# Start addresses and slot places of the MLP operands in an attention-then-two-MLPs kernel

## The chip, the core and the metric

One core of one Trainium2 chip runs the whole program. The metric is the device time of one execution in microseconds (us), as the median of several runs. Smaller is better.

## What is computed

The inputs are q, k and v of shape (4, 8, 576, 64) and four weight matrices. An attention with a feature map comes first, then two MLPs over 2,304 rows of 512 columns:

```python
def phi(x):
    proj = einsum('bhsd,df->bhsf', x, w_phi)
    proj = proj - max(abs(proj), axis=-1)
    return concatenate([exp(proj), exp(-proj)])
kv = einsum('bhsf,bhsd->bhfd', phi(k), v);  z = sum(phi(k), axis=2)
x = einsum('bhsf,bhfd->bhsd', phi(q), kv) / (phi(q) . z + 1e-06)     # (2304, 512)
h = x @ w1_in;  x = where(h > 0, h, exp(min(h, 0)) - 1) @ w1_out       # 512 -> 2048 -> 512
h = x @ w2_in;  out = (h * clip(h + 3, 0, 6) / 6) @ w2_out             # 512 -> 2048 -> 512
```

The MLP weights arrive as 64-bit floats and are turned into 32-bit floats on the chip. Every MLP product is made of three matmuls of the fp32r type on a high and a low part of each operand: high x high, low x high, high x low.

## The kernel before

**Order of work.** Nothing runs in the order of the source. Every piece of work is a `Step` with an engine, a duration that the program assumes, its predecessors, a rank, and tokens of rings (buffers). `in_order` plays them through and emits the instructions of each engine in the order that comes out. The engines then run their own queues in that order, and wait for each other by semaphores.

**Attention.** Eight units (`unit(u)`), each for two heads and two batches. A unit projects k and q in runs of eight tiles (`projs`, L312), subtracts the row maximum on DVE (L322, L336), exponentiates on ACT (L345, L408), sums keys times values on PE (L370), transposes q on PE (L395), multiplies (L429) and divides, with the quotient written into `x32` by POOL (`scale`, L476). All these matmuls are plain fp32. Each of L312, L370 and L429 stands in the trace as two matmul records per call.

**MLPs.** The 2,304 rows are cut into blocks: b = 0 to 3 have 512 rows, b = 4 has 256. The 16 slices f of 128 hidden columns are taken in groups of four (`M1_GROUPS`, `M2_GROUPS`): for each group all five blocks, for each block the four slices. One item is `hid` (L732, 12 matmuls into `ps_p`), then `act1`, `gate`, `gate_hi`, `gate_lo` on ACT and DVE (tiles `e`, `g`, `gh`, `gl`), then `outp` (L794, 12 matmuls, 6 in the second MLP for b = 4). On PE the `outp` of an item stands behind the `hid` of the next one. In `hid` the weights are the stationary operand and x the moving one. In `outp` of the first MLP the weights are stationary and `gh`, `gl` move; in the second MLP `gh`, `gl` are stationary and the weights move.

**Weights.** Slice w (0 to 31 over both MLPs) lives in slot j = w % 6, as `w_h` and `w_l` of 2 x 512 columns. `fetch` loads half a slice, DVE turns it into 32-bit parts in eight steps (`to_f32`, L661 to L673), POOL adds the last part (L678) into one of four `w_b` buffers, and `w_hi` (L700) and `w_lo` (L706) on POOL write the slot and free the buffer.

**Memory.** Tiles lie behind each other in the order in which pools are opened. Slots 0 and 1 are in `wra`, which is open from the start. Slots 2 and 3 are in `mlp_a`, which takes the place of `att_a` once its last user is done (`open_a`); slots 4 and 5 are in `mlp_b`, which takes the place of `att_b` (`open_b`).

```python
SLOT = ["wra", "wra", "a", "a", "b", "b"]
```

`xh` and `xl` of blocks 1 to 4 are tiles of KD x n columns (`new_x`), those of block 0 lie in the buffers of raw q and k (`first_x`). In the built program the starts, in bytes of a partition, are these (all starts of one row agree modulo 128):

| tiles | start modulo 128 |
|---|---|
| `w_h`, `w_l` of slots 0, 1, 4, 5; x of blocks 2, 3, 4 | 32 |
| `w_h`, `w_l` of slots 2, 3; x of blocks 0, 1; `gh`, `gl` | 96 |
| `e` and `st` of the attention (operands of L429) | 64 |
| `kp` of the attention (stationary operand of L370) | 96 |

Of the kernel before, what the change touches and what calls it, by code (L numbers as in the profile page):

```python
# [7 lines left out]

F32 = mybir.dt.float32
F32R = mybir.dt.float32r  # L10
I32 = mybir.dt.int32
I64 = mybir.dt.int64
AF = mybir.ActivationFunctionType
ALU = mybir.AluOpType
AX = mybir.AxisListType
# [122 lines left out]
def attention_then_two_mlps(  # L138
# [28 lines left out]
    B, S, D = 4, 576, 64  # L167
    NF = w_phi.shape[1] // 2
    NT, DM = out.shape
    DFF = w1_out.shape[0]  # L170
    R = S // 64
    KD = DM // 128
    FT = DFF // 128
# [32 lines left out]
    ov = x32.rearrange("p (t n) -> p t n", n=DM)  # L206
    half_c = const.tile([128, 1], F32, name="half_c")
    nc.gpsimd.memset(half_c, 0.5)


    sb = ExitStack()
# [383 lines left out]
    def open_a():  # L595
        sa.close()
        pools["a"] = ctx.enter_context(tc.tile_pool(name="mlp_a", bufs=1, side="right"))
        new_x("a", 1)

    def open_b():  # L600
        sb.close()
        pools["b"] = ctx.enter_context(tc.tile_pool(name="mlp_b", bufs=1))
        for b in range(2, NB):
            new_x("b", b)

    X = {}

    def new_x(pool_, b):
        t = [
            pools[pool_].tile([128, KD, blocks[b][1]], F32R, name=f"x{part}{b}") for part in "hl"  # L610
        ]
        X[b] = tuple([t_[:, kk] for kk in range(KD)] for t_ in t)

    def first_x():

        t = [
            [rawp.tile([128, 2, 512], F32R, tag=s_, name=f"x{part}0{i}") for i in range(2)]
            for part, s_ in (("h", "k"), ("l", "q"))
        ]
        X[0] = tuple([t_[kk // 2][:, kk % 2] for kk in range(KD)] for t_ in t)  # L620

    def y_open():
        pass
# [8 lines left out]
    }  # L632

    W, F = {}, {}
    SLOT = ["wra", "wra", "a", "a", "b", "b"]
    pools["wra"] = wra
    for j in range(len(SLOT)):
        rings[f"w{j}"] = 1
    rings.update({"s": 2, "ca": 1, "cb": WB, "el_e": 2, "el_r": 1, "el_g": 2, "el_gh": GB, "el_gl": GB,
                  "y0": 1, "y1": 1, "y2": 1, "y3": 1})  # L640

    def fetch(w, i):
        m, f = divmod(w, FT)
        w_in, w_out = ((w1_in, w1_out), (w2_in, w2_out))[m]
        s = stg.tile([128, 512], I64, tag="s", name="w64", bufs=2)
        if i == 0:
            nc.sync.dma_start(out=s, in_=w_in[f])
        else:
            nc.sync.dma_start(out=s, in_=w_out[f * 128:(f + 1) * 128, :])
        F[w, i] = s  # L650

    def to_f32(w, i):
# [86 lines left out]
    def act1(m, b, f):  # L739
        n = blocks[b][1]  # L740
        el = pools["a"]
        ps = H[m, b, f]
        e = el.tile([128, 512], F32, tag="e", name="e", bufs=2)
        if m == 0:
            r_ = el.tile([128, 512], F32, tag="r", name="r")
            nc.scalar.activation(out=r_[:, :n], in_=ps[:, :n], func=AF.Relu, scale=-1.0)  # L746
            nc.scalar.activation(out=e[:, :n], in_=r_[:, :n], func=AF.Exp, scale=-1.0)
        else:
            nc.scalar.activation(  # L749
                out=e[:, :n], in_=ps[:, :n], func=AF.Relu, scale=1.0 / 6.0, bias=half_c  # L750
            )
        G[m, b, f] = e
# [80 lines left out]
    for w in range(2 * FT):  # L833
        j = w % len(SLOT)
        WT[w] = Token(f"w{j}")
        for i in range(2):
# [1 line left out]
            ts_, ta, tb = Token("s"), Token("ca"), Token("cb")  # L838
            x = step("SP", 1.4, bind_(fetch, w, i), takes=[ts_], rank=lead - 5, behind=[chain] if chain else [])
            chain = x  # L840
            cost = [0.6, 0.33, 0.33, 0.33, 0.6, 0.6, 0.6, 0.31]
            fns = to_f32(w, i)
            for n_, (us, fn) in enumerate(zip(cost, fns)):
                x = step(
# [73 lines left out]
    for it in seq:  # L918
        m, begins, ends, fi, fn, b, f = it
        n = blocks[b][1]  # L920
        tp, te, tr, tg, th, tl = (Token(x) for x in ("p", "el_e", "el_r", "el_g", "el_gh", "el_gl"))
        gtok[m, b, f] = (th, tl)
        ready = xr[b] if m == 0 else [nexts[b, kk] for kk in range(KD)]
        s = step("PE", 12 * pe1(n), bind_(hid, m, b, f), after=[WL[m * FT + f, 0], *ready], rank=clock, takes=[tp],
                 uses=[WT[m * FT + f]])
        s.behind += [x for x in hids.get("last", [])]
        hids["last"] = [s]
        hids.setdefault((m, b), []).append(s)
        clock += 12 * pe1(n)
        when = clock  # L930
        s = step("ACT", act(n) * (1 + (m == 0)), bind_(act1, m, b, f), after=[s, OPEN["a"]], rank=when, uses=[tp],
                 takes=[te, tr] if m == 0 else [te])
        if m == 0:
            tr.users.append(s)
        s = step("DVE", dve(n), bind_(gate, m, b, f), after=[s], rank=when, uses=[te, tp], takes=[tg])
        s = step("ACT", act(n), bind_(gate_hi, m, b, f), after=[s], rank=when, takes=[th], uses=[tg])
        gl_of[m, b, f] = step("DVE", dve(n), bind_(gate_lo, m, b, f), after=[s], rank=when, takes=[tl], uses=[tg],
                              port=True)
        if prev is not None:
            put_outp(*prev, clock)  # L940
            clock += 12 * pe1(blocks[prev[5]][1])
        prev = it
# [16 lines left out]
def _laid_out(name, a):  # L959
# [7 lines left out]
    elif name == "w_phi":  # L967
        a = np.block([[a, np.zeros_like(a)], [np.zeros_like(a), a]])
    elif name.endswith("w_in"):
        a = a.reshape(4, 128, 16, 128).transpose(2, 1, 0, 3).reshape(16, 128, 512)  # L970
    return np.ascontiguousarray(a)


# [21 lines left out]
```

## Time and profile before

| | |
|---|---|
| median of 3 runs | 1015.91 us (1015.71 to 1016.2) |
| the profiled execution | 1015.86 us |
| its span | 1014.0 us |
| granted TensorE clock over the span | 0.998 |
| PE busy | 994.8 us |
| DVE / ACT / POOL busy | 728.0 / 422.2 / 281.4 us |

The span is the time from the first to the last instruction of the profiled execution, 1.9 us less than its own time. Times in the rows below count from the start of the span. A matmul is pipelined: its record is longer than the distance to the start of the next one, so the cost of one matmul is read from starts, or from the chain of work, whose pieces end where the next one begins.

### The profile page before, as it was taken

What the parts mean: (1) busy time and instruction counts of PE and PEld (TensorE: products, weight loads), DVE (VectorE), ACT (ScalarE), POOL (GpSimd) and SP (SyncE); (2) the same over time, 40 slices, a digit from 0 to 9 for tenths busy, and PEclk for the clock granted to TensorE, in tenths of its full rate; (3) what the DMA queues carried; (4) which work ended last, traced back from release to release, by engine and by line L of the source; (5) the groups of instructions that cost most, each with busy time, mean ns of one, the idle gap of its engine ahead of it and who ended that gap; (6) DMA issues with size and microseconds to landing.
All of it is one profiled execution on the core that took longest, in us unless ns stands there. A gap on an engine that the chain in (4) does not pass through costs nothing.

```text
span 1014.0 us, 13851 instructions
## 1 busy us (share of the span) xinstructions
PE 994.8 (98%) x5312; PEld 828.8 (82%) x5312; DVE 728.0 (72%) x1222; ACT 422.2 (42%) x815; POOL 281.4 (28%) x262
## 2 busy tenths in 40 slices
PE   8999999998999999999999999999999999999998
PEld 8887888877888888888888887888888888888886
DVE  4999986698928973997499949953995598743333
ACT  3777777873443333333335443333322222222222
POOL 2234211352205311431146445312421323130000
PEclk9999999999999999999999999999999999999999
DMA  8445440010201110111011101110121011001111
GB/s 213 106 105 121 118 115 2 1 42 22 85 20 42 63 63 1 43 63 63 1 42 63 62 2 42 62 63 1 55 71 42 1 42 63 21 1 42 42 42 63
DMA packets 33298, 53.45 MB, mean 53 GB/s; under 512 B 20304, under 2 KB 20432, under 8 KB 33232
## 3 DMA queue, kind: packets, MB, share of 16 engines
q1 hardware_dynamic: 33232, 52.57, 17.3%
q8 instruction: 42, 0.69, 0.3%
q14 instruction: 24, 0.20, 0.1%
HBM read 47.84 MB, written 4.72 MB: 52 GB/s over the span
## 4 chain that ended last, share of the span: by engine, by line
PE 89%; DVE 5%; ACT 4%; issue 1%; DMA 1%; POOL 0%; SPq 0%; ACTq 0%; POOLq 0%
PE ps_p L732 37%; PE ps_a L794 20%; PE ps_t L794 18%; PE ps_a L370 6%; PE ps_t L429 5%; PE ps_p L312 3%; ACT e L408 1%; DVE gl L775 1%; PE ps_t L395 1%; DVE xl L717 1%; ACT kp L345 1%; DMA raw_k<-in_k_dram 1%; DVE w_a L669 1%; ACT nd L444 1%; DVE w_b L673 0%
## 5 line engine op out<-in xcount | busy, mean ns | idle before, releaser
L732 PE MATMUL ps_p<-xh,w_h 128*128 128x512 f32 (+1 forms) x640 | 237.2, 371 | 0.0
L732 PE MATMUL ps_p<-xl,w_h 128*128 128x512 f32 (+1 forms) x640 | 236.8, 370 | 0.0
L732 PE MATMUL ps_p<-xh,w_l 128*128 128x512 f32 (+1 forms) x640 | 236.4, 369 | 0.0
L760 DVE SCALAR_TENSOR_TENSOR g<-e,ps_p 128x512 f32<-128x512 f32 (+1 forms) x160 | 101.0, 631 | 174.8 <-ACT e L749 116.4
L678 POOL TENSOR_TENSOR w_b<-w_b,w 128x512 int32<-128x512 int32 x64 | 90.3, 1410 | 291.9 <-DVE w L669 287.7
L775 DVE TENSOR_TENSOR gl<-g,gh 128x512 fp32r<-128x512 f32 (+1 forms) x160 | 121.9, 762 | 47.9 <-ACT gh L768 41.6
L749 ACT ACTIVATE e<-ps_p,half_c 128x512 f32<-128x512 f32 (+1 forms) x80 | 51.7, 646 | 229.7 <-PE ps_p L732 229.7
L768 ACT CAST gh<-g 128x512 fp32r<-128x512 f32 (+1 forms) x160 | 92.6, 579 | 120.5 <-DVE g L760 116.2
L732 PEld LDWEIGHTS ps_p<-xh,w_h 128*128 128x128 f32 x640 | 120.4, 188 | 22.5
L732 PEld LDWEIGHTS ps_p<-xl,w_h 128*128 128x128 f32 x640 | 120.4, 188 | 22.0
L732 PEld LDWEIGHTS ps_p<-xh,w_l 128*128 128x128 f32 x640 | 120.3, 188 | 21.5
L746 ACT ACTIVATE r<-ps_p 128x512 f32<-128x512 f32 (+1 forms) x80 | 44.5, 556 | 170.2 <-PE ps_p L732 170.1
L669 DVE TENSOR_SCALAR w_a<-w_a 128x512 int32<-128x512 int32 x128 | 98.8, 772 | 1.5
L700 POOL TENSOR_SCALAR w_h<-w_b 128x512 fp32r<-128x512 f32 x64 | 44.9, 702 | 177.8 <-PE ps_a L794 87.5
L673 DVE SCALAR_TENSOR_TENSOR w_b<-w,w_b 128x512 int32<-128x512 int32 x128 | 90.0, 703 | 2.5
L706 POOL TENSOR_TENSOR w_l<-w_b,w_h 128x512 fp32r<-128x512 f32 x64 | 87.5, 1368 | 4.9
L429 PE MATMUL ps_t<-e,st 128*128 128x256 f32 (+1 forms) x256 | 70.8, 419 | 4.3 <-ACT e L408 2.3
L370 PEld LDWEIGHTS ps_a<-vb,kp 128*128 128x128 f32 x576 | 67.9, 192 | 1.8 <-issue 0.2
L370 PE MATMUL ps_a<-vb,kp 128*128 128x130 f32 x576 | 69.1, 277 | 0.0
L476 POOL TENSOR_TENSOR x<-ns,rb 128x256 f32<-128x256 f32 (+1 forms) x32 | 28.1, 879 | 138.9 <-DVE rb L467 114.4
L794 PE MATMUL ps_a<-w_h,gl 128*128 128x512 f32 x160 | 63.4, 396 | 0.7 <-DVE gl L775 0.6
L794 PE MATMUL ps_a<-w_h,gh 128*128 128x512 f32 x160 | 63.2, 395 | 0.1
(72 smaller groups left out, 1724.5 us busy)
## 6 DMA issues: line engine op xcount, KB each, us to landing
w<-in_moe_w_in_dram SPq DMA_DIRECT2D x32, 512.0 KB, 3.5
w<-in_moe_w_out_dram SPq DMA_DIRECT2D x32, 512.0 KB, 3.5
vb<-in_v_dram SPq DMA_DIRECT2D x16, 288.0 KB, 5.4
out_dram<-x SPq DMA_DIRECT2D x18, 256.0 KB, 2.1
raw_k<-in_k_dram SPq DMA_DIRECT2D x7, 576.0 KB, 3.7
raw_q<-in_q_dram SPq DMA_DIRECT2D x7, 576.0 KB, 4.0
raw_k<-in_k_dram SPq DMA_DIRECT2D x1, 320.0 KB, 5.5
raw_q<-in_q_dram SPq DMA_DIRECT2D x1, 320.0 KB, 5.0
```

The source lines that it names most:

```text
L370: nc.tensor.matmul(out=acc[h][:, half].rearrange("p b d -> p (b d)"), lhsT=kp[:, i, half, :], rhs=vb[u % 2][:, r].rearrange("p h c -> p (h ...
L429: nc.tensor.matmul(out=ps[:, :n], lhsT=ST[h][:, half * 2 + bb, :], rhs=e[:, o:o + n], start=(half == 0), stop=(half == 1),)
L669: V.tensor_scalar(out=st[o], in0=st[x], scalar1=s1, scalar2=s2, op0=o1, **kw)
L673: return lambda: V.scalar_tensor_tensor(out=st["b"], in0=st[x], scalar=s1, in1=st["b"], op0=o1, op1=ALU.bitwise_or)
L678: nc.gpsimd.tensor_tensor(out=st["b"], in0=st["b"], in1=st["l"], op=ALU.add)
L706: nc.gpsimd.tensor_tensor(out=lo[:, i], in0=F.pop((w, i)), in1=hi[:, i].bitcast(F32), op=ALU.subtract)
L732: nc.tensor.matmul(out=ps[:, :n], lhsT=a_[:, 0, c], rhs=x_[kk], start=(i == 0), stop=(i == 3 * KD - 1),)
L749: nc.scalar.activation(out=e[:, :n], in_=ps[:, :n], func=AF.Relu, scale=1.0 / 6.0, bias=half_c)
L760: V.scalar_tensor_tensor(out=gt[:, :n], in0=e[:, :n], scalar=s, in1=ps[:, :n], op0=o0, op1=o1)
L768: nc.scalar.copy(out=gh[:, :n], in_=G[m, b, f][:, :n])
L775: V.tensor_tensor(out=gl[:, :n], in0=gt[:, :n], in1=gh[:, :n].bitcast(F32), op=ALU.subtract)
L794: nc.tensor.matmul(out=o, lhsT=a_, rhs=b_, start=(fi == 0 and i == 0), stop=(fi == fn - 1 and i == 2))
```

## The change

Weight slots 2 and 3 move into `wra`, which no longer waits for any pool of the attention; slot 4 goes to `mlp_a`, slot 5 stays in `mlp_b`. Three unused tiles (`gap_l`, `gap_r`, `gap_b`), a stride of 640 instead of 512 columns between the four parts of an x tile, and other places for block 0 set the start addresses. The tile `r` of `act1` goes: the exponential now reads and writes `e`. The second weight matrix of each MLP is handed over in the shape (16, 128, 512), with the same bytes in the same order. Two durations that `in_order` assumes for DVE rise (0.33 to 0.5 and 0.31 to 0.45).

In the built program the starts become:

| tiles | start modulo 128 | modulo 1,024 |
|---|---|---|
| `w_h`, `w_l` of all slots; `gh`, `gl` | 0 | 0 |
| x of blocks 0 to 3, part kk = 0, 1, 2, 3 | 0 | 512, 0, 512, 0 |
| x of block 4 | 0 | 0 |
| `e` and `st` of the attention | 32 | |
| `kp` of the attention | 0 | 0 |

```diff
+    const.tile([128, 344], F32, name="gap_l")
+    ctx.enter_context(tc.tile_pool(name="gap", bufs=1, side="right")).tile([128, 504], F32, name="gap_r")
...
         pools["a"] = ctx.enter_context(tc.tile_pool(name="mlp_a", bufs=1, side="right"))
-        new_x("a", 1)
+        new_x("a", 1, True)
...
         pools["b"] = ctx.enter_context(tc.tile_pool(name="mlp_b", bufs=1))
+        pools["b"].tile([128, 128], F32, name="gap_b")
         for b in range(2, NB):
-            new_x("b", b)
+            new_x("b", b, b == 3)
...
-    def new_x(pool_, b):
-        t = [
-            pools[pool_].tile([128, KD, blocks[b][1]], F32R, name=f"x{part}{b}") for part in "hl"
-        ]
-        X[b] = tuple([t_[:, kk] for kk in range(KD)] for t_ in t)
+    def new_x(pool_, b, last_=False):
+        n = blocks[b][1]
+        if n < 512:
+            t = [pools[pool_].tile([128, KD, n], F32R, name=f"x{part}{b}") for part in "hl"]
+            X[b] = tuple([t_[:, kk] for kk in range(KD)] for t_ in t)
+            return
+        x = []
+        for part in "hl":
+            size = KD * 640 - (128 if last_ and part == "l" else 0)
+            t = pools[pool_].tile([128, size], F32R, name=f"x{part}{b}")
+            x.append([t[:, kk * 640:kk * 640 + n] for kk in range(KD)])
+        X[b] = tuple(x)
...
     def first_x():
-        t = [
-            [rawp.tile([128, 2, 512], F32R, tag=s_, name=f"x{part}0{i}") for i in range(2)]
-            for part, s_ in (("h", "k"), ("l", "q"))
-        ]
-        X[0] = tuple([t_[kk // 2][:, kk % 2] for kk in range(KD)] for t_ in t)
+        t = {
+            (s_, i): rawp.tile([128, 1152], F32R, tag=s_, name=f"x0{s_}{i}") for s_ in "kq" for i in range(2)
+        }
+        def part(*where):
+            return [t[s_, i][:, o:o + 512] for s_, i, o in where]
+        X[0] = (
+            part(("k", 0, 640), ("q", 0, 0), ("q", 0, 640), ("k", 0, 0)),
+            part(("k", 1, 0), ("k", 1, 640), ("q", 1, 0), ("q", 1, 640)),
+        )
...
-    SLOT = ["wra", "wra", "a", "a", "b", "b"]
+    SLOT = ["wra", "wra", "wra", "wra", "a", "b"]
...
-            r_ = el.tile([128, 512], F32, tag="r", name="r")
-            nc.scalar.activation(out=r_[:, :n], in_=ps[:, :n], func=AF.Relu, scale=-1.0)
-            nc.scalar.activation(out=e[:, :n], in_=r_[:, :n], func=AF.Exp, scale=-1.0)
+            nc.scalar.activation(out=e[:, :n], in_=ps[:, :n], func=AF.Relu, scale=-1.0)
+            nc.scalar.activation(out=e[:, :n], in_=e[:, :n], func=AF.Exp, scale=-1.0)
...
-            cost = [0.6, 0.33, 0.33, 0.33, 0.6, 0.6, 0.6, 0.31]
+            cost = [0.6, 0.33, 0.33, 0.5, 0.6, 0.6, 0.6, 0.45]
```

**What moves.** SP issues the same loads in the same order. PE runs the same matmuls in the same order but for one place at the start of the MLPs. POOL and DVE differ.

On POOL, in the middle of the attention, before (`x32` is a unit's quotient, `w_b` the buffer of a half slice, `w_h`, `w_l` the slot):

```order
L678 TENSOR_TENSOR w_b_1055<-w_b_1055,w64_917 128x512
L476 TENSOR_TENSOR x32_74<-ns_1252,rb_1295 128x256
L476 TENSOR_TENSOR x32_74<-ns_1282,rb_1319 128x256
L678 TENSOR_TENSOR w_b_1186<-w_b_1186,w64_1106 128x512
L476 TENSOR_TENSOR x32_74<-ns_1321,rb_1361 128x320
L476 TENSOR_TENSOR x32_74<-ns_1376,rb_1417 128x320
```

and with the change:

```order
L692 TENSOR_TENSOR w_b_1060<-w_b_1060,w64_922 128x512
L714 TENSOR_SCALAR w_h2_1221<-w_b_1060 128x512
L720 TENSOR_TENSOR w_l2_1222<-w_b_1060,w_h2_1221 128x512
L478 TENSOR_TENSOR x32_74<-ns_1261,rb_1304 128x256
L478 TENSOR_TENSOR x32_74<-ns_1289,rb_1328 128x256
L692 TENSOR_TENSOR w_b_1191<-w_b_1191,w64_1111 128x512
L478 TENSOR_TENSOR x32_74<-ns_1330,rb_1370 128x320
L714 TENSOR_SCALAR w_h2_1221<-w_b_1191 128x512
L720 TENSOR_TENSOR w_l2_1222<-w_b_1191,w_h2_1221 128x512
L478 TENSOR_TENSOR x32_74<-ns_1385,rb_1426 128x320
```

The four pairs that fill slots 2 and 3, which stood behind the last `att_a` user, now stand inside the attention. Their `w_b` buffers come free there, and four more half slices (of slots 4 and 5) are worked on by DVE in the last two units of the attention.

On DVE, where the attention ends and blocks 2 to 4 of x are split, before:

```order
L661 TENSOR_SCALAR w_a_2535<-w64_2488 128x512
L669 TENSOR_SCALAR w_a_2535<-w_a_2535 128x512
L775 TENSOR_TENSOR gl_2554<-g_2407,gh_2548 128x512
L669 TENSOR_SCALAR w_a_2535<-w_a_2535 128x512
L717 TENSOR_TENSOR xl2_2561<-x32_74,xh2_2560 128x512 x4
L717 TENSOR_TENSOR xl3_2563<-x32_74,xh3_2562 128x512 x4
L717 TENSOR_TENSOR xl4_2565<-x32_74,xh4_2564 128x256 x2
L775 TENSOR_TENSOR gl_2622<-g_2499,gh_2615 128x512
```

and with the change (`gl_2650` is of the same item as `gl_2554` before, `gl_2676` of the same as `gl_2622`):

```order
L683 TENSOR_SCALAR w64_2253<-w64_2253 128x512
L455 STREAM_TRANSPOSE t1_2579<-nd_2555 128x320
L461 RECIPROCAL rr_2582<-t1_2579 128x10
L469 STREAM_TRANSPOSE rb_2584<-rr_2582 128x320
L731 TENSOR_TENSOR xl2_2606<-x32_74,xh2_2605 128x512 x4
L788 TENSOR_TENSOR gl_2650<-g_2470,gh_2630 128x512
L731 TENSOR_TENSOR xl3_2608<-x32_74,xh3_2607 128x512 x4
L731 TENSOR_TENSOR xl4_2610<-x32_74,xh4_2609 128x256 x2
L788 TENSOR_TENSOR gl_2676<-g_2573,gh_2660 128x512
```

Three weight steps in front of the split are gone, and the `gl` of slice 2 now stands behind four `xl` steps. On PE, the `hid` of block 1 with slot 1 stands ahead of the `outp` with slot 2 instead of behind it.

## Rows read from the trace of the kernel before

**Rows 1.** The page: busy time of each engine, share of the span, instructions.

```profile
PE 994.8 (98%) x5312; PEld 828.8 (82%) x5312; DVE 728.0 (72%) x1222; ACT 422.2 (42%) x815; POOL 281.4 (28%) x262
```

**Rows 2.** The page: the chain of waits, by engine and by line.

```profile
PE 89%; DVE 5%; ACT 4%; issue 1%; DMA 1%; POOL 0%; SPq 0%; ACTq 0%; POOLq 0%
PE ps_p L732 37%; PE ps_a L794 20%; PE ps_t L794 18%; PE ps_a L370 6%; PE ps_t L429 5%; PE ps_p L312 3%; ACT e L408 1%; DVE gl L775 1%; PE ps_t L395 1%; DVE xl L717 1%; ACT kp L345 1%; DMA raw_k<-in_k_dram 1%; DVE w_a L669 1%; ACT nd L444 1%; DVE w_b L673 0%
```

**Rows 3.** Busy time by stretch: stretch, length, then PE, PEld, DVE, ACT, POOL.

```profile
307.90:1010.10 702.20, 701.00 (x3276) 580.20 (x3275) 488.97 (x777) 222.28 (x383) 195.11 (x167) 1.00 0.12 41
51.30:75.80 24.50, 23.34 (x194) 19.77 (x192) 22.69 (x46) 18.41 (x42) 7.36 (x8) 1.00 0.41 98
149.90:174.30 24.40, 23.51 (x195) 19.99 (x194) 15.00 (x33) 18.24 (x43) 3.20 (x4) 1.00 0.12 16
```

**Rows 4.** The chain of waits in time: start, length (us), engine, tile, line, count.

```profile
236.87 2.72 PE ps_p L732 x12
...
250.52 2.73 PE ps_p L732 x12
...
261.52 2.79 PE ps_p L732 x12
...
289.25 2.80 PE ps_p L732 x12
...
299.01 1.43 PE ps_p L732 x12
300.44 0.71 PE ps_a L794 x6
...
301.86 1.39 PE ps_p L732 x12
...
317.59 2.75 PE ps_p L732 x12
```

**Rows 5.** Fp32 matmuls: a timeline row, a row by line, a row of the chain.

```profile
84.33 2.32 PE L429 MATMUL ps_t<-e,st 128*128 128x320 f32 x8
...
L429 PE MATMUL ps_t<-e,st 128*128 128x320 f32 x128 | 38.1, 439 | 0.2 <-ACT ns L448 0.2
...
189.97 4.58 PE ps_a L370 x41
```

**Rows 6.** Timeline at the end of the attention, POOL, DVE and PE; then PE's waits.

```profile
222.82 1.07 POOL L476 TENSOR_TENSOR x<-ns,rb 128x320 f32<-128x320 f32 x1
...
226.56 7.09 DVE L717 TENSOR_TENSOR xl<-x,xh 128x512 fp32r<-128x512 f32 x10
233.56 0.68 DVE L775 TENSOR_TENSOR gl<-g,gh 128x512 fp32r<-128x512 f32 x1
...
234.30 0.50 PE L794 MATMUL ps_a<-gl,w_h 128*128 128x512 f32 x1 [2.62 <-DVE gl L775]
...
PE ps_a L794 <- DVE gl L775: 3.5, 3, 2.6
```

**Rows 7.** The chain of waits in time through one item of the 256-row block.

```profile
303.33 0.39 ACT r L746
...
303.74 0.43 ACT e L747
...
304.19 0.43 DVE g L760
...
304.65 0.42 ACT gh L768
...
305.09 1.31 DVE gl L775
...
306.44 0.74 PE ps_a L794 x4
```

More of the change, by code (lines that the diff above doesn't have):

```diff
@@ L9 @@
 F32 = mybir.dt.float32
+I64 = mybir.dt.int64
 F32R = mybir.dt.float32r
 I32 = mybir.dt.int32
-I64 = mybir.dt.int64
 AF = mybir.ActivationFunctionType
@@ L169, in attention_then_two_mlps @@
     NT, DM = out.shape
-    DFF = w1_out.shape[0]
+    DFF = w1_out.shape[0] * w1_out.shape[1]
     R = S // 64
@@ L638, in attention_then_two_mlps @@
         rings[f"w{j}"] = 1
-    rings.update({"s": 2, "ca": 1, "cb": WB, "el_e": 2, "el_r": 1, "el_g": 2, "el_gh": GB, "el_gl": GB,
+    rings.update({"s": 2, "ca": 1, "cb": WB, "el_e": 2, "el_g": 2, "el_gh": GB, "el_gl": GB,
                   "y0": 1, "y1": 1, "y2": 1, "y3": 1})
@@ L645, in fetch @@
         s = stg.tile([128, 512], I64, tag="s", name="w64", bufs=2)
[L646 to L649, printed above, removed]
+        nc.sync.dma_start(out=s, in_=(w_in, w_out)[i][f])
         F[w, i] = s
@@ L920, in attention_then_two_mlps @@
         n = blocks[b][1]
-        tp, te, tr, tg, th, tl = (Token(x) for x in ("p", "el_e", "el_r", "el_g", "el_gh", "el_gl"))
+        tp, te, tg, th, tl = (Token(x) for x in ("p", "el_e", "el_g", "el_gh", "el_gl"))
         gtok[m, b, f] = (th, tl)
@@ L931, in attention_then_two_mlps @@
         s = step("ACT", act(n) * (1 + (m == 0)), bind_(act1, m, b, f), after=[s, OPEN["a"]], rank=when, uses=[tp],
-                 takes=[te, tr] if m == 0 else [te])
-        if m == 0:
-            tr.users.append(s)
+                 takes=[te])
         s = step("DVE", dve(n), bind_(gate, m, b, f), after=[s], rank=when, uses=[te, tp], takes=[tg])
@@ L970, in _laid_out @@
         a = a.reshape(4, 128, 16, 128).transpose(2, 1, 0, 3).reshape(16, 128, 512)
+    else:
+        a = a.reshape(16, 128, 512)
     return np.ascontiguousarray(a)
```

## The prediction

> **What bounds the kernel now.** I read the page first, for the engine that is full: PE is busy 98% of the span, DVE 72% [rows 1]. The chain of waits then says that this is no accident of averages: 89% of the chain is PE, and 37 + 20 + 18 = 75% is the two lines of the MLPs, L732 and L794 [rows 2]. The busy time by stretch shows a steady stage from the start of the second group at 307.90 us to the end: 3276 matmuls in 702.20 us, PE busy for 701.00 of them [rows 3]. So nothing but the price of a matmul, and the few places where PE stands still, can move the end by more than a few us.
>
> That price is read in the chain in time, where a piece of 12 matmuls ends as the next begins. The reader should put each piece beside the start addresses of its two operands modulo 128. In the first two rows of [rows 4] both operands have the same remainder (x of block 1 with slot 2, 96 and 96; x of block 2 with slot 0, 32 and 32): 2.72 and 2.73 us, 227 ns each. In the last row x of block 0 (96) meets slot 0 (32): 2.75 us, 229 ns. At 261.52 and 289.25 x (32) meets slots 2 and 3 (96): 2.79 and 2.80 us, 233 ns. The work is the same, so the addresses set the price. In cycles of 2.4 GHz, which the granted clock of 1.00 [rows 3] gives, 512 columns need 512 and take 544, 550 and 560. The 256-row block shows the same in small: 1.43 / 12 = 119 ns with 32 and 32, 1.39 / 12 = 116 ns with 32 and 96 [rows 4]; 119.2 ns is 286 cycles for 256 columns. In the like case the surplus is 30 to 32 cycles for 256 columns and for 512, so it is a price per matmul and not per column.
>
> **The matmuls, term 1.** All MLP operands start at multiples of 512 after the change. No fp32r matmul of the trace has such a start, so the new price needs bounds. From below: eight fp32 records of 320 columns, whose operands start at 64 modulo 128, take (2.32 - 0.439) / 7 = 269 ns from start to start [rows 5]. At two cycles a column that is 267 ns of streaming and 2 ns besides; by it 512 columns of fp32r would cost 213.3 + 2 to 2.5 = 216 ns, and 256 columns 109 to 110. From above, among starts: 233 ns, the worst pair [rows 4]. One row speaks for a small effect: 41 records of L370, 130 columns with a stationary operand at 96, take 4.58 / 41 = 112 ns against 108 of streaming, 3.4 ns besides [rows 5], so a start off 64 costs fp32 little more than 1 ns. [...] A surplus of 32 cycles is what one piece of 128 bytes more takes at one 4-byte column a cycle, and a tile of 2,048 bytes that starts at 32 or 96 touches 17 such pieces instead of 16. That is my reading of 544 = 17 x 32 and of some 288 = 9 x 32; the trace doesn't prove it. I take 216 and 110 ns, the nearest case with clean starts, for the likeliest, and keep 233 as the upper end.
>
> How much that is: the steady stage has 2784 matmuls of 512 columns and 492 of 256 by the code (7 groups). Less 492 x 118 ns = 58.1 us, 702.2 us leaves 231.3 ns for each of the 512 kind, waits included. By pairs, with the counts of the code (1272 alike at 226.7, 1008 at 229, 888 at 233.4) the mean is 229.3. I use 230.2, between them. Over the whole program 3168 x (230.2 - 216) = 45.0 us and 576 x (118 - 110) = 4.6 us: **49.6 us off**. All of it lies on PE, so on the path.
>
> The Trainium skill, SBUF — State Buffer, section Who interferes with whom, speaks against this term: TensorE has two independent read ports, for the moving operand and for the weight load, and "PE and ACT never wait on anyone". By that rule no pair of addresses can cost more than another, and the change would gain nothing here but the small terms below. The trace disagrees: 2.72 against 2.80 us for the same 12 matmuls, by the pair alone [rows 4].
>
> **The slots, term 2.** POOL's four pairs of `w_hi` and `w_lo` for slots 2 and 3 move into the attention, and DVE works on four more half slices there. A unit loaded with such work took 24.50 us with DVE busy for 22.69; an unloaded one took 24.40 with DVE at 15.00 [rows 3]. Two units become loaded: +0.2 us. At the end of the attention DVE has three weight steps less before the split of x. Now it runs ten `xl` steps of 7.09 us from 226.56 and only then the `gl` for which PE stands still for 2.62 us [rows 6]. The split cannot start much sooner, since the last quotient comes from POOL only at 222.82 + 1.07 and ACT must copy it first [rows 6]. But a `hid` of 2.7 us moves ahead of that `outp` on PE and covers part of the wait. I take -1.5 us, between -2.6 (the wait goes) and +2 (the `gl` of slice 2, now behind four `xl` steps of 0.7, becomes late as well).
>
> **The shorter cover, term 3.** An item of the 256-row block takes PE 24 x 118 ns = 2.83 us; its chain from the first `ACT` to the end of `gl` is 303.33 to 306.40, 3.07 us, and PE stands still for a moment there [rows 7]. With 110 ns an item has 2.64 us, so each late `gl` waits 0.2 us longer. There are 32 such items: 0 to 6 us. I take +2.5, one and a half late items a group. Items of 512 rows have 24 x 216 = 5.2 us of cover and are safe.
>
> **The rest.** `e` and `st` of L429 move from 64 to 32 modulo 128: by L370's surplus 256 x 1.4 ns = +0.4 us; at most 256 x 13 ns = 3.4 us, if a whole piece were paid. The exponential in place of `e` saves a buffer and no instruction; the new shape of the second weights moves the same bytes; the gap tiles run nothing: 0, on engines that PE covers. The two assumed durations only reorder DVE, 0 within the bounds of term 2.
>
> **Sum.** -49.6 + 0.2 - 1.5 + 2.5 + 0.4 = -48.0. The profiled execution took 1015.86 us, 0.05 under the median of the runs shown, so that **967.9 us** is the forecast for either.
>
> **The rivals.** (A) One piece of 16 columns stays. 544 and 560 are 512 plus two and three times 16 cycles [rows 4], so the surplus may be two causes of 16 cycles, a start off the grid and a meeting of the two reads, and only the first goes. Then 528 cycles, 220 ns: 3168 x 10.2 + 576 x 2 = 33.5 us off, with -1 for the rest 981 us. For it: the pairs differ, so something besides the start of one operand counts. (B) Only the relation of the two operands counts, and all pairs become alike: 226.7 and 119 ns, so 3168 x 3.5 - 576 x 1 = 10.5 us off, with -1.5 for the slots 1004 us. For it: fp32 hardly cares for its start [rows 5]. Against it: it leaves the 32 cycles unexplained. (C) Slower: equal starts make the weight load and the moving read meet more often, and every pair becomes as dear as the worst one, 233.4 ns: 3168 x 3.2 = +10.1 us, with -1 for the rest 1025 us. It decides as soon as the mean of a 512-column matmul passes 230.6 ns. For it: which remainders meet now makes 6 ns either way. Against it: like remainders are the cheap case today [rows 4]. (D) Nothing changes for the matmuls, and the slots give -1.5: 1014.4 us, which lies within 0.2%, about what a measurement of this kernel can tell from no change. The Trainium skill, SBUF — State Buffer, section Specifications (TRN2), gives cachelines of 16 bytes; every start before is a multiple of 16 already, so by that rule the new starts change nothing, which is this case. The differing pairs in [rows 4] disagree with it.
>
> **How the numbers follow.** The forecast gets 0.51, A 0.20, B 0.17, C 0.08, D 0.04. Its own range is 957 (no surplus at all, the wait at 234 us gone) to 974 (term 3 at 6 us, L429 at its bound). For 8 in 10 I reach over A and B and leave out C and D and the tails: 957 to 1006 us. Faster by over 0.2%: 0.51 + 0.20 + 0.17 = 0.88; within it: 0.04; slower: 0.08.
>
> **What would show it.** In the chain in time of the changed kernel, 12 matmuls of `ps_p` with 512 columns should take 2.59 us (A: 2.64; B: 2.72; C: 2.80), whatever the slot and block, and 12 of 256 columns 1.32. L429's row should stay near 269 ns from start to start. The wait of `ps_a` for `gl` at the end of the attention should be under 2.6 us, and the waits in the 256-row block a few tenths longer than now. The forecast is wrong if pieces of 12 still differ by slot, if they are alike at 2.72 or more, or if the 256-row block waits for over 1 us per group.

## The result and the profile after

The changed kernel takes 1007.16 us (median of 4 runs, 1004.17 to 1007.3) where the kernel before takes 1016.06 beside it: a ratio of 0.9904, 95% interval 0.9884 to 0.9923. It is faster, by 8.9 us instead of the 48.0 of the forecast, and the time lies 1.2 us above the range that was given. The profiled execution took 1007.1 us, with a span of 1005.3.

First the page of the changed kernel: engines, and the chain of waits by engine and by line (L746 is the old L732, L807 the old L794).

```profile
PE 986.8 (98%) x5312; PEld 829.9 (83%) x5312; DVE 718.1 (71%) x1222; ACT 422.7 (42%) x815; POOL 280.4 (28%) x262
...
PE 91%; ACT 4%; DVE 4%; issue 0%; POOL 0%; POOLq 0%; ACTq 0%
```

Against [rows 1, 2] nothing has changed places: PE is still busy 98% of the span and makes up 91% of the chain. So the question is again the price of a matmul. The chain of waits in time (start, length, engine, tile, line, count) answers it:

```profile
239.01 2.72 PE ps_p L746 x12
...
282.53 2.72 PE ps_p L746 x12
...
300.47 1.44 PE ps_p L746 x12
...
316.17 2.72 PE ps_p L746 x12
```

Of the 111 pieces of 12 matmuls with 512 columns in this chain from 235 us on 102 take 2.72 us, whichever slot and block: 226.7 ns each. The other nine take 2.73 to 2.75. The spread of [rows 4], 2.72 to 2.80, is gone, but nothing fell below its lowest row. The pieces of the 256-row block, 1.39 and 1.43 before, are now all at 1.43 to 1.45: 119 to 121 ns each.

Busy time by stretch of the changed kernel (stretch, length, PE, PEld, DVE, ACT, POOL, then the granted clock): the steady stage, then three stretches up to the first MLP item.

```profile
306.36:1001.22 694.86, 692.89 (x3278) 580.81 (x3276) 488.18 (x776) 222.99 (x383) 195.66 (x167) 1.00 0.12 42
...
0.00:10.00 10.00, 6.30 (x48) 5.78 (x48) 3.18 (x6) 2.55 (x4) 5.45 (x18) 0.99 0.79 176
10.00:17.00 7.00, 6.46 (x40) 6.03 (x42) 4.18 (x7) 2.57 (x5) 0.00 (x0) 0.53 1.11 275
17.00:197.44 180.44, 173.54 (x1442) 148.37 (x1441) 163.05 (x332) 133.62 (x305) 55.98 (x56) 1.00 0.39 101
```

The steady stage shrank from 702.20 us [rows 3] to 694.86. The third row shows where some of it went again: between 10 and 17 us the granted clock was 0.53 on average, so most of this stretch ran at the lower of its two levels (1.2 and 2.4 GHz). The same stretch of the kernel before:

```profile
10.00:17.00 7.00, 6.33 (x57) 5.89 (x57) 4.85 (x9) 3.38 (x7) 0.00 (x0) 0.76 1.14 272
```

0.53 against 0.76 means 57 matmul records before, 40 after in these 7 us. In both, PE stood still for almost 3 us before 10.7 us, in the first projections. The one run of the changed kernel whose clock was 1.000 throughout took 1004.17 us; the other three, at 0.996 and 0.997, took 1007.1 to 1007.3.

From the starts of all matmul records of the two profiled executions the account is this. A matmul counts from its start to the next start; one whose next start comes late is counted at the price of the others, and what is left is a wait. Where that line is drawn moves an entry by up to 0.3 us and a difference by 0.1.

| | before, us | after, us |
|---|---|---|
| 3168 matmuls of 512 columns, without waits | 729.3 | 719.1 |
| 576 matmuls of 256 columns, without waits | 68.2 | 69.2 |
| waits inside the MLPs | 7.4 | 6.6 |
| what begins with a matmul of the attention | 203.2 | 204.6 |

The sum is -10.2 + 1.0 - 0.8 + 1.4 = -8.6, against -8.7 in the spans.

The first entry can be split by pairs of starts, when each record is put beside the starts that its two operands have in the built program:

| stationary operand ahead of the moving one, bytes modulo 256 | matmuls of 512 columns before | mean ns before | mean ns after |
|---|---|---|---|
| 0 | 1272 | 228.5 | 227.1 (all 3168) |
| 64 | 888 | 233.3 | none left |
| 192 | 1008 | 229.9 | none left |

So 5.5 of the 10.2 us come from the pairs 64 apart, 2.8 from those 192 apart, and 1.8 from pairs that were alike already. In the series below a pair needs some matmuls until its price is steady, which would fit this last part: in the kernel before, like pairs follow unlike ones. The waits show in PE's list (waited for: us in total, times, longest) and in the timeline at their two main places:

```profile
PE ps_a L807 <- DVE gl L788: 2.4, 3, 1.1
...
PE ps_p L314 <- DVE mx L324: 2.9, 1, 2.9
```

```profile
232.79 0.68 DVE L788 TENSOR_TENSOR gl<-g,gh 128x512 fp32r<-128x512 f32 x1
233.52 0.50 PE L807 MATMUL ps_a<-gl,w_h 128*128 128x512 f32 x1 [0.67 <-DVE gl L788]
...
538.08 1.33 POOL L720 TENSOR_TENSOR w_l<-w_b,w_h 128x512 fp32r<-128x512 f32 x1
538.20 1.76 DVE L788 TENSOR_TENSOR gl<-g,gh 128x512 fp32r<-128x512 f32 x1
540.01 0.50 PE L807 MATMUL ps_a<-gl,w_h 128*128 128x512 f32 x1 [1.09 <-DVE gl L788]
```

At the end of the attention PE's wait for `gl` fell from 2.62 us [rows 6] to 0.67. A new one of 1.09 us stands at 538 us: the `gl` step, which took 0.68 us at 232.79 with POOL idle, takes 1.76 here, and ends 0.55 us after POOL's `w_lo`.

### The profile page after: what moved, and what is told of

It is laid out like the page before. It is cut to its first block, busy times and chain, and to the rows that moved or that the text cites. A ratio compares the mean times of both kernels' runs of the same rounds, so it can differ in the third digit from the quotient of the medians.

```text
span 1005.3 us, 13762 instructions
## 1 busy us (share of the span) xinstructions
PE 986.8 (98%) x5312; PEld 829.9 (83%) x5312; DVE 718.1 (71%) x1222; ACT 422.7 (42%) x815; POOL 280.4 (28%) x262
## 4 chain that ended last, share of the span: by engine, by line
PE 91%; ACT 4%; DVE 4%; issue 0%; POOL 0%; POOLq 0%; ACTq 0%
PE ps_p L746 37%; PE ps_a L807 20%; PE ps_t L807 18%; PE ps_a L372 7%; PE ps_t L431 5%; PE ps_p L314 3%; ACT e L410 1%; PE ps_t L397 1%; DVE xl L731 1%; DVE gl L788 1%; ACT kp L347 1%; ACT e L419 1%; ACT nd L446 1%; DVE x L820 0%; ACT ns L450 0%
## 5 line engine op out<-in xcount | busy, mean ns | idle before, releaser
L746 PE MATMUL ps_p<-xh,w_h 128*128 128x512 f32 (+1 forms) x512 | 185.7, 363 | 0.0
L746 PE MATMUL ps_p<-xh,w_l 128*128 128x512 f32 (+1 forms) x512 | 185.6, 362 | 0.0
L746 PE MATMUL ps_p<-xl,w_h 128*128 128x512 f32 (+1 forms) x512 | 185.6, 362 | 0.0
L788 DVE TENSOR_TENSOR gl<-g,gh 128x512 fp32r<-128x512 f32 (+1 forms) x160 | 124.5, 778 | 50.5 <-ACT gh L781 47.6
L759 ACT ACTIVATE e<-ps_p 128x512 f32<-128x512 f32 (+1 forms) x80 | 44.5, 556 | 167.9 <-PE ps_p L746 167.9
L746 PEld LDWEIGHTS ps_p<-xh,w_h 128*128 128x128 f32 x512 | 96.6, 189 | 16.0
L746 PEld LDWEIGHTS ps_p<-xl,w_h 128*128 128x128 f32 x512 | 96.5, 189 | 15.9
L746 PEld LDWEIGHTS ps_p<-xh,w_l 128*128 128x128 f32 x512 | 96.6, 189 | 15.0
L683 DVE TENSOR_SCALAR w_a<-w_a 128x512 int32<-128x512 int32 x128 | 89.0, 695 | 1.4
L807 PE MATMUL ps_a<-w_h,gl 128*128 128x512 f32 x160 | 62.6, 391 | 0.7 <-DVE gl L788 0.6
L807 PE MATMUL ps_a<-w_h,gh 128*128 128x512 f32 x160 | 62.6, 391 | 0.1
L431 PEld LDWEIGHTS ps_t<-e,st 128*128 128x128 f32 x256 | 44.9, 189 | 21.6 <-ACT ns L450 5.7
```

The source lines that it names most:

```text
L431: nc.tensor.matmul(out=ps[:, :n], lhsT=ST[h][:, half * 2 + bb, :], rhs=e[:, o:o + n], start=(half == 0), stop=(half == 1),)
L683: V.tensor_scalar(out=st[o], in0=st[x], scalar1=s1, scalar2=s2, op0=o1, **kw)
L746: nc.tensor.matmul(out=ps[:, :n], lhsT=a_[:, 0, c], rhs=x_[kk], start=(i == 0), stop=(i == 3 * KD - 1),)
L788: V.tensor_tensor(out=gl[:, :n], in0=gt[:, :n], in1=gh[:, :n].bitcast(F32), op=ALU.subtract)
L807: nc.tensor.matmul(out=o, lhsT=a_, rhs=b_, start=(fi == 0 and i == 0), stop=(fi == fn - 1 and i == 2))
```

## The experiments

**Which price belongs to which starts.** Behind the last item, where all other engines are done, 28 series of 20 equal matmuls were added to the changed kernel (`w4` and `w5` are the high parts of two weight slots, both starting at 0 modulo 1,024):

```diff
+    PROBES = [(512, 128, o, s) for o, s in (...)] + [(n, 128, 0, 0) for n in (384, 256, 128)] + ...
+    for n, m, o, s in PROBES:
+        ps = bank("p")
+        for i in range(20):
+            nc.tensor.matmul(out=ps[:m, :n], lhsT=w4[:, s:s + m], rhs=w5[:, o:o + n], ...)
```

> The changed kernel with 28 extra series of 20 fp32r matmuls behind its last item, when all other engines are done: moving operand and weights at chosen start offsets (weights off by 16 to 1024 bytes, moving operand off by 16 to 512 bytes, both off alike), then fewer columns, then narrower weights. Their results go nowhere. Theory 1 (the relation of the two starts sets the price, because the weight load and the moving read meet): series with both starts equal, or both off by 32, take 226.7 ns from start to start; series with a difference of 64 bytes take 229 to 234; some difference takes under 224; narrower weights take less than 226.7. Theory 2 (a fixed price of about 32 cycles for every fp32r matmul, on which the relation only adds): no series of 512 columns with 128 weight columns is under 224 ns, and narrower weights change nothing. Theory 3 (other engines' reads add the surplus): the equal series take 216 ns here, where nobody else reads.

Busy time by stretch, each stretch one series from its first start to the next one's (stretch, length, PE, clock). In order: moving and weights both at 0; weights 64, 96, 192, 256 bytes further; moving 64 bytes further; both at 32; 256 columns, both at 0.

```profile
1000.87:1005.41 4.54, 4.54 (x21) 1.00 0.31 117
1014.61:1019.28 4.67, 4.67 (x22) 1.00 0.02 4
1019.28:1023.96 4.68, 4.68 (x22) 1.00 0.00 0
1028.61:1033.20 4.59, 4.59 (x21) 1.00 0.00 0
1033.20:1037.75 4.55, 4.55 (x21) 1.00 0.00 0
1060.77:1065.35 4.58, 4.58 (x22) 1.00 0.00 0
1083.78:1088.34 4.56, 4.56 (x22) 1.00 0.00 0
1105.64:1108.02 2.38, 2.38 (x21) 1.00 0.00 0
```

Once steady that is 226.6, 233.6, 234.6, 228.8, 226.6, 228.9, 226.6 and 120.0 ns. Weights 64 bytes ahead cost 233.6, 64 bytes behind 228.9, the same as 192 ahead: the difference counts, with a period of 256 bytes. Both at 32 is as cheap as both at 0. Nothing goes below 226.6, which is 544 cycles at 2.4 GHz; 384 columns settle at 416 cycles and 256 at 288, so the surplus of 32 is one per matmul. It does not go on below that: 128 columns took 111.8 ns, 268 cycles and not 160, and the series don't say what sets this price. Weights of 96, 64 or 32 columns instead of 128 made 512 columns no cheaper (230 to 232 ns), so a shorter weight load doesn't lessen the surplus. Theory 1 is right on the relation, but no difference came under 224 ns. Theory 3 fell: the equal series took 226.6 ns and not 216 with nobody else at work. Theory 2 fits, a fixed 32 cycles on which the relation adds, but for the narrower weights, which should have changed nothing. A clean start of each operand is not needed.

**Starts alone and slots alone.** The changed kernel with the old places of the slots, and the kernel before with the new ones:

```diff
-    SLOT = ["wra", "wra", "wra", "wra", "a", "b"]
+    SLOT = ["wra", "wra", "a", "a", "b", "b"]
```

> The changed kernel with the slots back where they were (two in the pool that is open from the start, two in each of the others), all starts still multiples of 512. If the starts are all of the gain, about 1007 to 1009 us: the matmuls as in the changed kernel (12 in 2.72 us everywhere), the wait for gl at the end of the attention back at 2.6 us. If the slots carry half of it, 1011 us or more.

> The kernel before with four slots in the pool that is open from the start, starts as before. By the counts of the pairs the mean price of a 512-column matmul stays (229.4 against 229.3 ns). If the slots matter by the wait alone: 1014 to 1015 us, with the wait for gl at the end of the attention at 1 us or less. If they are part of the main gain: 1011 us or less. If the attention's last two units pay for the work moved into them: 1016 us or more.

Starts alone: 1007.1 us, ratio 0.9906 (0.9888 to 0.9924). Slots alone: 1015.03 us, ratio 0.9991 (0.998 to 1.0002). The starts are all of the gain that can be measured. PE's timeline at the end of the attention shows what the slots do, first with the starts alone:

```profile
231.98 0.50 PE L807 MATMUL ps_a<-gl,w_h 128*128 128x512 f32 x1 [1.96 <-DVE gl L788]
```

and with the slots alone:

```profile
230.99 0.50 PE L794 MATMUL ps_a<-gl,w_h 128*128 128x512 f32 x1 [0.56 <-DVE gl L775]
```

The wait for `gl` there is 1.96 us with the old slots (2.62 in the kernel before, where 2.6 was expected back) and 0.56 with the new slots (0.67 in the changed kernel): term 2's mechanism is there, 1.3 to 2 us in size. In the kernel with slots alone the matmuls of 512 columns took 0.3 ns more each, waits left out. The moved slots meet x at other differences: by the starts in the built program 1026 instead of 1272 are alike. That takes 1 us back.

**The start of the program.** More warm-up matmuls in the changed kernel:

```diff
-    WARM = 16
+    WARM = 32
```

> The changed kernel with 32 instead of 16 dummy transposes ahead of the attention. In the changed kernel three of four runs have a granted clock of 0.996 to 0.997 and take 1007.1 to 1007.3 us, one has 1.000 and takes 1004.17. If the difference is the clock falling to its lower level in the first 17 us, in the pause while the first loads land, and more dummy work bridges that pause: runs near 1004 to 1005 us at 1.000. If the difference comes from elsewhere, or the dummies end before the pause: 1007 us again, or the dummies delay the first projection and it is 1008 us.

1005.84 us (1005.64 to 1005.97), ratio 0.9897 (0.988 to 0.9913). Busy time by stretch:

```profile
10.00:17.00 7.00, 5.97 (x58) 5.17 (x59) 7.00 (x12) 3.77 (x8) 0.00 (x0) 1.00 1.10 265
```

The clock is granted in full, 58 records run instead of 40, and the first MLP item starts at 196.08 us instead of 197.44. The five runs lie within 0.33 us of each other; the four of the changed kernel spread over 3.1. The median is between the two that were expected (1004 to 1005, and 1007), for the longer warm-up has a price of its own: the first projection starts at 7.52 us instead of 4.98, and none of the five runs comes near the 1004.17 us that the changed kernel took once at full clock. The same stretch of two other runs with 16 warm-up matmuls, the slots alone, and the shifted 256-row block that is described below:

```profile
10.00:17.00 7.00, 6.38 (x71) 6.05 (x72) 5.88 (x12) 2.79 (x6) 0.00 (x0) 1.00 1.23 285
10.00:17.00 7.00, 6.43 (x57) 5.99 (x58) 4.96 (x9) 3.38 (x7) 0.00 (x0) 0.76 1.13 268
```

With 16 warm-up matmuls, what begins with a matmul of the attention took 201.9 us at 1.00 (the slots alone, on the same chip as the runs with 32), 203.2 to 203.8 in the five profiled runs at 0.76, and 204.5 to 205.0 in the four at 0.51 to 0.53. With 32 at full clock it took 203.2. The kernel before and three kernels with the changed starts stand within 0.1 us of each other at 0.76. So the 1.4 us that the attention lost are the clock's level in these first microseconds and not the change's addresses. Most of the scatter is that too: in 17 runs of the kernel before on one chip the five with a clock of 1.000 took 1013.69 to 1014.10 us, and the four at 0.994 and 0.995 took 1018.04 to 1018.66. What decides whether the clock falls isn't shown. In the run of the slots alone PE stood still for 3.27 us at the same place, and it stayed in full.

**Is the surplus one of the type?** More series, with fp32 and bf16 operands in place of fp32r (`f4` and `f5` are the two slots read as fp32, `b5` is a tile filled with bf16), and finer differences of the starts:

```diff
+    PROBES = [(w5, w4, 256, 128, 0, s) for s in range(0, 64, 4)] + ...
+    PROBES += [(f5, f4, 512, 128, 0, s) for s in (0, 16, 32)] + [(f5, f4, 256, 128, 0, 0)]
+    PROBES += [(b5, b5, 512, 128, 0, 512 + s) for s in (0, 16, 32, 48)] + [(b5, b5, 256, 128, 0, 512)]
```

> The changed kernel with 36 series of 20 matmuls behind its last item, read from start to start once a series is steady. Three questions. (1) Moving 256 columns, with the weights' start 0 to 240 bytes further in steps of 16. Theory R (the relation of the two starts counts, with a period of 256 bytes): the price depends on the difference; the kernel before had 113.3 ns at a difference of 64 and 118 to 119 ns at 0, so some differences should give 113 and the like case 120. Rival S (113 in the kernel before had another cause, such as the gaps in its 256-row block): 120 at all differences, or more. (2) 512 columns at odd multiples of 16 bytes: R expects values between 226.6 and 234.6 ns and none under 226; a value under 222 would say that a better place exists. (3) Is the surplus of 32 cycles (13.3 ns) a matmul a property of the type? If it belongs to fp32r, plain fp32 of 512 columns takes 427 to 431 ns and bf16 of 512 columns 213 to 217 ns. If it belongs to every matmul whatever its type, fp32 takes 440 or more (or 453, if each of its passes pays it) and bf16 226.6 ns.

Busy time by stretch. In order: fp32, 512 columns, like starts and 64 bytes apart (each call is two records, so 40 in a stretch); bf16, 512 columns, like starts and 32 bytes apart; bf16, 256 columns to the last matmul but one; fp32r, 256 columns, like starts and weights 64 bytes ahead.

```profile
1081.50:1098.66 17.16, 17.16 (x41) 1.00 0.00 1
1098.66:1115.83 17.17, 17.17 (x42) 1.00 0.00 0
...
1141.63:1145.94 4.31, 4.31 (x21) 1.00 0.01 4
1145.94:1150.26 4.32, 4.32 (x21) 1.00 0.00 0
1158.89:1161.07 2.18, 2.18 (x21) 1.00 0.00 0
999.68:1002.05 2.37, 2.37 (x21) 1.00 0.55 207
1009.14:1011.41 2.27, 2.27 (x22) 1.00 0.00 0
```

One fp32 record of 512 columns takes 429.2 ns (1024 + 6 cycles), one bf16 matmul 215.8 (512 + 6), at every difference tried. The fp32r matmul takes 512 + 32 at best, and alone depends on its starts. This decides the case: 216 ns was a right price for a type that the MLPs don't use. The Trainium skill, TensorE: Matmul & The Clock Gate, section Back-to-back issue gap, gives N / 2.4 + 2.5 ns as the gap of a single matmul of N columns at the full clock. In the series here bf16 agrees with that (215.8), and fp32r doesn't (226.6).

For 256 columns of fp32r one difference is cheaper than the like case: 113.4 ns (272 cycles) with the weights 64 bytes ahead. The others lie between 116 and 120. For 512 columns the odd multiples of 16 bytes took 226.6 to 233.6 ns, so there is no better place than the like one.

**The new wait at 538 us.** The changed kernel with the two assumed durations of before:

```diff
-            cost = [0.6, 0.33, 0.33, 0.5, 0.6, 0.6, 0.6, 0.45]
+            cost = [0.6, 0.33, 0.33, 0.33, 0.6, 0.6, 0.6, 0.31]
```

> The changed kernel with the two assumed DVE durations put back to 0.33 and 0.31, so that only the order of DVE's and POOL's steps differs. Theory P (the wait of 1.1 us that PE has for gl at about 538 us in the changed kernel comes from the order that these durations give): that wait is gone, and the time falls by about 1 us, to 1006. Rival Q (it comes from POOL's work that fell beside these gl steps through the freer slots): the wait stays or moves, and the time is within 0.5 us of the changed kernel's.

1004.04 us (1002.6 to 1006.01), ratio 0.9868 (0.9849 to 0.9887). Timeline at the same place, and PE's waits:

```profile
536.69 1.29 POOL L720 TENSOR_TENSOR w_l<-w_b,w_h 128x512 fp32r<-128x512 f32 x1
...
537.41 1.12 DVE L788 TENSOR_TENSOR gl<-g,gh 128x512 fp32r<-128x512 f32 x1 [0.69 <-ACT gh L781]
...
PE ps_a L807 <- DVE gl L788: 1.3, 2, 0.7
```

POOL's step now ends about half a microsecond into `gl`, which takes 1.12 us instead of 1.76, and PE's stop is gone, as theory P has it: 2.4 us of waits in three places became 1.3 in two. The wait came from the order that the two higher durations give. The account of the matmul starts gives 1.6 us for it; the rest of the 3 us between the medians is within the scatter that the start of the program gives both. In both runs `gl` ends 0.55 us after POOL's `w_lo`, however early it began. The Trainium skill, SBUF — State Buffer, section Who interferes with whom, says that a DVE step with two inputs in SBUF contends with a POOL step that reads SBUF, and that the one that comes second waits. The 1.76 and 1.12 us, against 0.68 beside an idle POOL, agree.

**Alike, or clean?** Every operand of the changed kernel 32 bytes further on:

```diff
-    const.tile([128, 344], F32, name="gap_l")
-    ... .tile([128, 504], F32, name="gap_r")
+    const.tile([128, 352], F32, name="gap_l")
+    ... .tile([128, 496], F32, name="gap_r")
```

> The changed kernel with both gaps changed by eight columns, so that every MLP operand starts 32 bytes further on: all at 32 modulo 128 where they were at 0, and their relation to each other as before. Theory R (only the relation counts): the same time as the changed kernel within 0.3% (1004 to 1008 us), 226.9 ns for a clean matmul of 512 columns. Rival T (the clean start of each operand gives something, as the forecast had it): the gain of about 10 us goes wholly or in part, 1010 to 1016 us, and 512 columns take 229 ns or more.

1006.1 us (1005.73 to 1007.2), ratio 0.99 (0.9885 to 0.9916). Its chain in time:

```profile
302.59 1.44 PE ps_p L746 x12
...
320.85 2.72 PE ps_p L746 x12
```

The gain is all there with no MLP operand on a clean start, and rival T falls. "Aligned" is the wrong word for the change: what it does is make the starts alike.

**The cheaper difference for 256 columns.** The moving operands of the 256-row block 192 bytes further:

```diff
+    OFF = {(m, b): 48 if (m, blocks[b][1]) == (0, 256) else 0 for m in range(2) for b in range(NB)}
...
+        gh = gh[:, OFF[m, b]:OFF[m, b] + n]
...
+            t = pools[pool_].tile([128, 2 * KD * n + 64], F32R, name=f"x{b}")
+            X[b] = tuple([t[:, 48 + (p * KD + kk) * n:48 + (p * KD + kk + 1) * n] for kk in range(KD)] for p in range(2))
```

> The changed kernel with the moving operands of the 256-row block started 192 bytes further (x4 in both MLPs, gh and gl in the first), so that the weights stand 64 bytes ahead of them modulo 256. Theory R: each of the 576 matmuls of 256 columns takes 113.4 ns instead of 120, as in the series; 576 x 6.6 = 3.8 us less on PE, of which the waits for gl at the end of this block give back up to 1 us: 1003 to 1004.5 us beside 1007 for the changed kernel. Rival U (113.4 holds only in a series that uses one pair of operands over and over): under 1 us is gained, and a matmul stays at 118 to 120 ns.

1003.17 us (1002.28 to 1004.98), ratio 0.9871 (0.9849 to 0.9892). The time is the one that theory R gave, but not for its reason: the matmuls took 117.7 ns, close to U's 118 to 120 and not 113.4, so only 1 us of the 3.8 came. The spans differ by 3.2 us: about 1 is this, about 1 lies in the 512-column matmuls (those of `outp` took 0.4 ns less each, and the runs don't show why), and 1.2 in the attention, where the granted clock between 10 and 17 us was 0.76 instead of 0.53. To see why 117.7, a third set of series ran the 256 columns with other slots, and with the operands changing as in `hid`. `SAME` keeps one pair of operands; `MOVE`, `SLICE` and `PARTS` change the moving tile, the columns of the weights, or the weights' tile; `HID` changes all three as in an item:

```diff
+    PROBES = [(256, j, p, 0, 16) for p in (SAME, HID) for j in (4, 0, 1, 2, 3)]
+    PROBES += [(256, 4, p, 0, 16) for p in (MOVE, SLICE, PARTS)]
+    PROBES += [(256, 4, HID, 0, s) for s in range(0, 64, 4) if s != 16] + [(256, 4, HID, 48, 0)]
+    PROBES += [(512, 4, HID, 0, s) for s in (0, 16, 32, 60)]
```

> The changed kernel with 33 series of 24 matmuls behind its last item, to find why 256 columns with the weights 64 bytes ahead take 113.4 ns in the earlier series and 117.8 ns in the kernel with the shifted 256-row block. Theory V (what counts is a change of operands from one matmul to the next): the series with one pair stays at 113.4 ns whatever the slot of the weights, and a series that changes the moving tile, the weights' tile or the slice of columns is at 117 to 118, as are all those in the order of the hid item. Rival W (the distance of the two tiles in memory counts beyond 256 bytes): the one-pair series differ by slot, 113.4 ns for slot 4 and 117 to 118 for some of slots 0 to 3, and the hid order with slot 4 stays at 113.4. Third (the other engines slow the reads in the running kernel): all series, also those in the hid order, are at 113.4. For 512 columns in the hid order: 226.6 ns at 0 and 240 bytes, 233 at 64 and 128, as with one pair.

Busy time by stretch, 24 matmuls each, in the order of `hid`: 256 columns with the weights 64, 0 and 192 bytes ahead; 512 columns with 0 and 64.

```profile
1013.33:1016.04 2.71, 2.71 (x26) 1.00 0.00 0
1035.09:1037.96 2.87, 2.87 (x26) 1.00 0.03 6
1066.47:1069.30 2.83, 2.83 (x27) 1.00 0.03 6
1080.52:1085.97 5.45, 5.45 (x26) 1.00 0.01 3
1085.97:1091.57 5.60, 5.60 (x26) 1.00 0.00 0
```

Alone, the order of `hid` takes 113.4 ns as well, for all five slots, so theories V and W fell. (512 columns with the weights 240 bytes ahead took 228.4 ns here, where 226.6 was expected.) The third theory, that the other engines slow the reads in the running kernel, isn't needed. The trace of the kernel before has ten items whose 256-column weights stand 64 bytes ahead, in the first stretch below with POOL at work beside it; both stretches are 12 matmuls of such an item:

```profile
902.29:903.65 1.36, 1.36 (x13) 1.00 0.00 0
304.43:305.84 1.41, 1.41 (x14) 1.00 0.00 0
```

Six of the ten items come to 113 or 114 ns from start to start within six matmuls. The other four stay at 117 to 119, in the mean about 117.7. The kernel with the shifted block stays there throughout, also in the first MLP, where 72 such matmuls follow each other. So one difference of starts has two steady prices, 113.4 and 117.7. A series shows how late a price can settle: with the moving operand at 192 and the weights at 0, as in the shifted block, the first five took 119, 116, 118, 122 and 119 ns and all later ones 113 or 114. What decides between the two prices stays open.

**All three together.** Block 4 shifted, the durations of before and 32 warm-up matmuls:

> The changed kernel with three edits: the 256-row block's moving operands 192 bytes further, the assumed DVE durations back at 0.33 and 0.31, and 32 instead of 16 warm-up matmuls. If the gains add: 1007.1 - 3.3 (block 4) - 1.4 (the wait at 538 us) - 1.4 (the start) = 1001 us. If the three compete for the same slack, 1002.5 to 1004.

1002.22 us (1002.18 to 1002.61), ratio 0.9861 (0.9847 to 0.9876): the lowest median, though its interval overlaps with those of the last two versions, and four runs within 0.43 us. Stretches of it:

```profile
10.00:17.00 7.00, 6.05 (x59) 5.25 (x60) 7.00 (x12) 3.85 (x8) 0.00 (x0) 1.00 1.12 267
...
304.69:996.34 691.65, 690.60 (x3278) 580.06 (x3276) 489.39 (x776) 222.32 (x383) 195.65 (x167) 1.00 0.13 42
```

Full clock at the start, 3.2 us less in the steady stage than the changed kernel. The time lies between the two that were expected. The 1001 us had counted the clock twice, in the 3.3 us of block 4 (1.2 of them) and in the 1.4 of the start. Counted once, the gains come to 4.9 us, and the spans differ by 4.9.

## Why the prediction was wrong

**What bounds the kernel** was read rightly: PE, by the price of a matmul, and the spread of [rows 4] came from pairs of starts.

**Term 1 failed**, in the sentence "I take 216 and 110 ns, the nearest case with clean starts, for the likeliest". The clean case came from fp32 records [rows 5]: their surplus of 2.4 ns was right for fp32 (429.2 ns for 512 columns here), and the step that carried it over to fp32r was not. Every fp32r row of 512 columns in the trace showed 32 cycles or more, at like starts too, and the text explained this by the offset from a clean start ("one piece of 128 bytes more"). A row that could have tested it was missing, and the 17 x 32 was a fit to two numbers. The runs showed in its place that an fp32r matmul with like starts carries exactly 32 cycles, once settled, for 256, 384 and 512 columns, and carries them for 512 columns at clean starts and with both operands at 32 or at 64 bytes alike. No run shows a read in pieces of 128 bytes. With 227.0 instead of 216 ns the 45.0 us shrink to 10.2; with 120 instead of 110 the 4.6 turn into 1.0 the other way. The base of the sum was right: 230.2 ns were taken for a matmul of 512 columns, and 729.3 / 3168 is 230.2 (the quotient in the text is 231.4, not 231.3, which changes nothing).

The objection that was set aside is the rule of the Trainium skill, SBUF — State Buffer, section Who interferes with whom, with its two independent ports. It held a part of the truth. It does not hold for fp32r here, where pairs differ by 8 ns with all other engines idle. For fp32 and bf16 the same series show no difference.

**Rival B** had the mechanism: only the relation counts, all pairs at 226.7 and 119, 1004 us. Measured 1007.16, on a profiled execution of 1007.1. The 3.2 us between are, but for 0.2 of rounding, the matmuls (-9.2 instead of -10.5 us: 1.3), the waits (-0.8 instead of -1.5: 0.7), and the clock at the start of the attention (1.4). At full clock the kernel ran in 1004.17; that this meets B's 1004 is luck, since the 1015.86 from which B starts was itself a run with a granted clock of 0.76 in the stretch from 10 to 17 us. "Against it: it leaves the 32 cycles unexplained" was the reason for its 0.17; a surplus without an explanation was no evidence against a relation that explained every difference.

**Rival A** (528 cycles), **C** (all pairs as dear as the worst) and **D** (starts don't matter) did not come. Against D, the kernel with starts alone took 0.9906 of the time, though every start before was a multiple of 16 bytes already.

**Term 2** was right in place and size at the end of the attention: 2.62 to 0.67 us, -1.5 forecast. What was late next lay elsewhere, at 538 us, from the durations that the forecast put at "0 within the bounds of term 2". The two, of opposite sign, left -0.8 in all the MLPs. The +0.2 us for the work that moves into the attention fits the 203.2 and 203.3 us that it took before and after at the same granted clock. Slots alone are worth nothing measurable.

**Term 3** fell with term 1: the matmuls of the 256-row block got dearer, not cheaper, so its cover grew. In the first MLP the matmul that waits for `gl` at the end of this block started 0.39 to 0.48 us after the one ahead of it in the kernel before, and 0.32 us in the changed one. The link that the term used is real: with the shifted block's cheaper matmuls this distance was 0.36 to 0.37 us again.

**L429** cost nothing by its new starts, where +0.4 was forecast: its matmuls of 320 columns start 269 ns apart in both kernels. The 1.4 us more in the attention came from the granted clock, since the kernel with the shifted block, with the same starts there and the clock of the kernel before, is back at 203.3 us.

## What to carry to other kernels

A bound for a price must come from the same type of instruction: one row of fp32 said nothing of fp32r, and a series of 20 matmuls behind the kernel would have told it in one run. Where a cost depends on addresses, vary one operand and then both together before calling it alignment; for fp32r with 512 columns here the starts of the moving operand and the weights should be alike modulo 256 bytes, wherever they are. And read the first 20 us by their granted clock before explaining a difference of 1 to 3 us by the change.

## What the hardware showed that was not expected

- An fp32r matmul of 256 columns or more carries 32 cycles besides its columns (226.6 ns for 512, 120.0 for 256, like starts), bf16 and fp32 records 6 (215.8 and 429.2 ns for 512). What the 32 cycles are isn't shown; fewer weight columns don't lessen them. With 128 columns it is 268 cycles (111.8 ns) in all.
- Of the three types only fp32r depends on its starts (fp32 was tried at three differences, bf16 at four). Moving 512 columns took 226.6 ns at a difference of 0 modulo 256 bytes in every series, and 228 to 235 ns at all others but two, with the other engines idle. At those two the price is not a fixed one: weights 16 bytes ahead took 226.6 ns in one series and 233.4 in another, and 240 bytes ahead 226.6, 228.4 and 231.2.
- For 256 columns the cheapest difference is another one: 113.4 ns with the weights 64 bytes ahead, 120.0 with like starts. Inside a running kernel the same difference settles at 113.4 or at 117.7.
- Twice the warm-up matmuls kept the clock at full level through the start in the profiled run and cut the scatter of the runs from 3.1 to 0.3 us. They also delayed the first projection by 2.5 us: at full clock what begins with a matmul of the attention took 203.2 us with 32 of them and 201.9 with 16.
